# Second layer: the weight words' absolute value moved from ScalarE to VectorE, and a ring of eight tiles for results that DMA adds to DRAM

## The chip, the cores and the metric

The kernel runs on one core of a Trainium2 chip. The metric is the device time of one execution in microseconds, the median of several runs. The kernel before takes 573.15 us (three runs, 572.9 to 574.02).

## The reference

Retention-like attention over 768 steps feeds two feed-forward layers in a row, all in fp32:

```python
state = gamma * state + k_t (outer) v_t            # batch 2, heads 8, head_dim 64
y_t = scale * q_t @ state
x = y as (1536 tokens, 512)
h = x @ w_in;  x = (h * clip(h + 3, 0, 6) / 6) @ w_out         # first layer, d_ff 2048
h = x @ w_in2; out = (h * tanh(softplus(h))) @ w_out2          # second layer, d_ff 2048
```

The weights reach the kernel as 64-bit words. On the chip, five elementwise steps make an fp32 tile from the two 32-bit halves of each word.

## The kernel before

Tokens form three blocks of 512, of which blocks 1 and 2 are mostly worked on together. A product in near-fp32 accuracy is three matmul passes over a high and a low part of each operand; ScalarE casts the high part ("gh", "wdh", "wsh": a CAST) and VectorE subtracts to get the low part ("gl", "wdl", "wsl"). Quadrants of the matrices are combined so that a pair of blocks (or two halves of block 0) needs seven products in place of eight ("up_pair", line 774, "pair_down", line 954).

The second layer (layer 1) runs from about 300 us to the end, in four groups g of two weight pairs each. A group has an **up stage**, in which the products go to the PSUM tiles wx and wy, and a **down stage**, in which they go to the PSUM tiles acc. In the up stage ScalarE copies a first product out of wx or wy (the snap, line 811), VectorE adds others to it (line 814), and ScalarE applies Mish (line 731) in place or straight from PSUM. Products of a pair of blocks are 512 columns wide ("w"); those of block 0 are 256 wide ("v"). TensorE cannot reuse wx before the snap has left it. The down stage has two parts, "block" (b) and "pair" (p); AFTER (line 58) says for each group which comes first.

The down stages of groups 0 to 2 leave 16 results each, four from the block and twelve from the pair. ScalarE copies each out of acc ("copied", line 921; 48 copies in all) into one of four tiles, sb00 to sb03 in turn. From there a DMA writes it to a DRAM tile "part": the first time plainly, from SP's queue (line 933, 12 DMAs), later with an addition, from GpSimd's queue (line 935, 36 DMAs). Two of a group's copies get another product added in the tile by VectorE (line 927) before they leave. A copy into an sb tile therefore waits until the DMA of the copy four before it has read that tile. Two results of each group are joined by VectorE in the sb tile before they leave (line 927).

While a group runs, the weights of the next are prepared: two halves per pair, "cvu" for up and "cvd" for down. Each half starts with the absolute value of the high words, an ACTIVATE with function Abs on ScalarE (line 444), followed on VectorE by a clamp (446), a shift with mask (448) and two merges with the raw words (449, 451). One cvu, one cvd and two raw buffers exist. Abs and Mish are in different function tables here: in the second layer an ACT_TABLE_LOAD stands wherever ScalarE goes from the one to the other.

The order of all instructions is made by a planner ("Plan.order", line 130): each step has an engine, an estimated time, its inputs, its buffers and a rank, and the engine takes the ready step of the lowest rank. ScalarE, VectorE, GpSimd and SP run their own queues strictly in that order, so a step that waits holds up those behind it.

Of the kernel before, what the change touches and what calls it, by code (L numbers as in the profile page):

```python
# [11 lines left out]
F32 = mybir.dt.float32  # L12
# [3 lines left out]
AF = mybir.ActivationFunctionType  # L16
ALU = mybir.AluOpType
# [3 lines left out]
P = 128  # L21
# [33 lines left out]
FREE = 1.5  # L55
ISSUE, ADDED = 1.0, 5.7
ORDER = (1, 5, 6, 3, 7, 2, 4)
AFTER = ("bp", "bp", "pb", "pb")
BORDER = {"pb": (2, 3, 0, 1), "bp": (0, 1, 2, 3)}
KPV = 1  # L60

# [1 line left out]
def dve(n, two=True):  # L63
    return 0.15 + n * (1.045e-3 if two else 0.525e-3)


def act(n, bias=False):
    return 0.17 + n * 0.86e-3 + (0.09 if bias else 0.0)
# [30 lines left out]
class Plan:  # L99
# [3 lines left out]
    def add(self, nm, eng, dur, deps, bufs, emit, rank=None):  # L103
        bufs = list(dict.fromkeys(getattr(b, "base", b) for b in bufs))
        t = Task(nm, eng, dur, deps, bufs, emit, rank)
        t.idx = len(self.tasks)
        self.tasks.append(t)
        for b in bufs:
            if not b.users:
                t.new.append(b)  # L110
                b.owner = t
            elif b.owner not in t.deps:
                t.deps.append(b.owner)
            b.users.append(t)
        for d in t.deps:
            d.succ.append(t)
        return t
# [87 lines left out]
def body(ctx: ExitStack, tc: tile.TileContext, aps: dict, out: bass.AP):  # L205
    nc = tc.nc
# [3 lines left out]
    fix = ctx.enter_context(tc.tile_pool(name="fix", bufs=1))  # L210
# [12 lines left out]
    def buf(pool, shape, tag, dt=F32):  # L223
        count[0] += 1
        name = f"{tag}_{count[0]}"

        def make():
            if pool == "post" and "post" not in pools:
                att.close()
                pools["post"] = ctx.enter_context(tc.tile_pool(name="post", bufs=1, reuse_waits="tile"))  # L230
            return pools[pool].tile(shape, dt, tag=tag, name=name, bufs=BUFS.get(tag, 1))
        return Buf(tag, make)
# [7 lines left out]
    V, A = nc.vector, nc.scalar  # L240
    pl = Plan()
    add = pl.add
# [29 lines left out]
    for n, what in enumerate(LOADS.split() + [f"{x}{u}" for u in range(NU) for x in ("qk", "kv")]  # L272
# [4 lines left out]
        elif what[0] == "t":  # L277
            if what not in lds:
                c = int(what[1:])
# [62 lines left out]
    def seq(key, us):  # L342
        pe_rank[key] = clock[0]
        clock[0] += us
# [16 lines left out]
    def sq_up(u):  # L361
        seq(u, {"c": 12 * MMR, "w": 6 * MMR, "v": 6 * MMH}[u[0]])
        up_end[u] = clock[0]
# [28 lines left out]
    for g in range(NG):  # L392
        for nxt in flow1[g]:
            sq_up(nxt)
        for what in AFTER[g]:
            if what == "b":
                for f in range(g * 2 * NP, (g + 1) * 2 * NP):
                    for d in BORDER[AFTER[g]]:
                        seq(("bd", f, d), 3 * MMR)
# [20 lines left out]
    def words_of(layer, p, half, cb, parts):  # L420

        rb = buf("fix", [P, 1024], "raw", I64)
        src = aps["w1" if layer == 0 else "w2"][p, half]

        def part(k):
            n = 1024 // parts
            cs = slice(k * n, (k + 1) * n)
            nm = f"w{layer}_{p}_{half}{k}"
            ld = add(nm, "SP", DMA512 * n / 512, [], [rb],
                     lambda: nc.sync.dma_start(out=rb.tile[:, cs], in_=src[:, cs]))  # L430
            ld.after = ld_w[0]
            ld_w[0] = ld

            def words():
                w = rb.tile.bitcast(I32).rearrange("p (n t) -> p n t", t=2)
                return w[:, cs, 0], w[:, cs, 1]

            def c():
                return cb.tile[:, cs]

            def ci():
                return cb.tile.bitcast(I32)[:, cs]
            a0 = add(nm + "abs", "ACT", act(n), [ld], [rb, cb],
                     lambda: A.activation(c(), words()[1].bitcast(F32), AF.Abs))  # L444
            a1 = add(nm + "c", "DVE", dve(n, False), [a0], [cb],
                     lambda: V.tensor_scalar(c(), c(), TOP_MAX, TOP_MIN, ALU.min, ALU.max))
            a2 = add(nm + "t", "DVE", dve(n, False), [a1], [cb],
                     lambda: V.tensor_scalar(ci(), ci(), 3, 0x3FFFFFF8, ALU.logical_shift_left, ALU.bitwise_and))
            a3 = add(nm + "o1", "DVE", dve(n), [a2], [cb, rb], lambda: V.scalar_tensor_tensor(
                out=ci(), in0=words()[0], scalar=29, in1=ci(), op0=ALU.logical_shift_right, op1=ALU.bitwise_or))  # L450
            return add(nm + "o2", "DVE", dve(n), [a3], [cb, rb], lambda: V.scalar_tensor_tensor(
                out=ci(), in0=words()[1], scalar=-0x40000000, in1=ci(), op0=ALU.bitwise_and, op1=ALU.bitwise_or))
        return part
# [76 lines left out]
    xt, x32, tform = {}, {}, {}  # L530
# [386 lines left out]
    added = {}  # L917
    taken = [0]
    back = {}

    def copied(nm, ac, dep, rk):
        taken[0] += 1
        tp = buf("fix", [P, 512], f"sb0{taken[0] % 4}")
        return tp, add(f"ev{nm}", "ACT", act(512), [dep], [ac, tp], lambda: A.copy(tp.tile, ac.tile), rk)  # L924

    def joined(nm, ac, tp, cs, deps, rk):
        return add(f"ev{nm}", "DVE", dve(cs.stop - cs.start), deps, [ac, tp], lambda: V.tensor_tensor(
# [2 lines left out]
    def into_part(nm, tp, b, d, dep):  # L930
        pt = part[b, d]
        if (b, d) not in added:
            added[b, d] = add(f"pw{nm}", "SP", 0.8, [dep], [tp, pt], lambda: nc.sync.dma_start(out=pt.tile, in_=tp.tile))
        else:
            added[b, d] = add(f"pa{nm}", "POOL", ADDED, [dep, added[b, d]], [tp, pt], lambda: nc.gpsimd.dma_start(  # L935
                out=pt.tile, in_=tp.tile, accum_op=ALU.add))

    def read_back(b):
# [15 lines left out]
    def pair_down(g):  # L954
# [34 lines left out]
        def rank_after(k, d):  # L989
            later = [pe_rank["pd", g, n, ps[0], d] for n in ORDER[ORDER.index(k) + 1:] if banks[n] == banks[k]]  # L990
            if not later and AFTER[g] == "bp":
                return up_end[flow1[g][-1]] + 40.0
            return (later[0] if later else pe_rank["bd", ps[0] * 2, banks[k][d]]) - DVE1 - LAT
        for k in ORDER:
# [21 lines left out]
            for d in range(2):  # L1016
                ac, rk, nm = accs[banks[k][d]], rank_after(k, d), f"{g}_{k}_{d}"
                dd = 2 * half + d
                if final:
                    into_back(nm, ac, b, dd, [last[d]], rk, k in (3, 7, 2, 4))  # L1020
                    ev[banks[k][d]] = back[b, dd][1] if k not in (3, 7, 2, 4) else []
                elif k == 3:
                    tp, t = kept[d]
                    t = joined(nm, ac, tp, slice(0, 512), [last[d], t], rk)
                    into_part(nm, tp, b, dd, t)
                else:
                    tp, t = copied(nm, ac, last[d], rk)
                    ev[banks[k][d]] = [t]
                    if k == 6:
                        kept[d] = (tp, t)  # L1030
                    else:
                        into_part(nm, tp, b, dd, t)

    def block_down(g):
        fs = range(g * 2 * NP, (g + 1) * 2 * NP)
        final = g == NG - 1
        accs = [buf("acc", [P, 512], f"acc{d}") for d in range(4)]
        prev = {}
        for f in fs:
            gb, tg = gval[1, f, 0]  # L1040
            gh, gl, tl = split(f"b{f}", gb, tg)
            wh, wl, wt = wdown[1, f]
            for d in BORDER[AFTER[g]]:
                ends = f == NFT - 1 and d == 1
                for n, cs in enumerate((slice(0, 256), slice(256, 512)) if ends else (slice(0, 512),)):
                    prev[d, n] = add(f"B{f}_{d}{n}", "PE", 3 * (MMH if ends else MMR), [tl, wt, prev.get((d, 0))],
                                     [wh, wl, gh, gl, accs[d]], lambda d=d, cs=cs, f=f, wh=wh, wl=wl, gh=gh, gl=gl: passes(
                                         accs[d], wh, wl, d * P, gh, gl, f == fs[0], f == fs[-1], cs),
                                     pe_rank["bd", f, d] + 0.36 * n)
                    if f == fs[-1] and final:  # L1050
                        into_back(f"b{f}_{d}{n}", accs[d], 0, d, [prev[d, n]], None, True, cs)
        if not final:
            for d in BORDER[AFTER[g]]:
                rk = pe_rank["pd", g, ORDER[d // 2], g * NP, d % 2] - DVE1 - LAT
                if AFTER[g] == "pb":
                    rk += 33.0
                tp, t = copied(f"b{g}_{d}", accs[d], prev[d, 0], rk)
                into_part(f"b{g}_{d}", tp, 0, d, t)
# [107 lines left out]
```

## Time and profile before

| | |
|---|---|
| median of three runs | 573.15 us |
| the profiled execution, its time | 574.66 us |
| its span on the core | 572.9 us |
| PE (TensorE) busy | 542.8 us, 95% |
| DVE (VectorE) busy | 467.8 us, 82% |
| ACT (ScalarE) busy | 367.7 us, 64% |
| POOL (GpSimd) busy | 34.3 us, 36 adding DMAs |
| mean granted clock of TensorE | 0.987 |

Busy time is the sum of instructions of an engine. "Idle before" of an instruction is how long its engine stood still ahead of it, and the name behind the arrow is what ended that wait by the profile. [...] Neighbouring instructions of one engine overlap a little, so the distance from one start to the next counts, not the duration.

### The profile page before, as it was taken

The numbers are of one execution on the slowest core, as the hardware profiler recorded it, in microseconds if no ns is written. First come the engines' busy times: TensorE is split into PE (matmuls) and PEld (weight loads), VectorE is DVE, ScalarE is ACT, GpSimd is POOL, SyncE is SP. The second block draws the span as 40 slices with busy tenths as digits, with TensorE's granted clock in tenths as the row PEclk, the third lists the DMA queues.
The fourth block names the chain that finished last, engine by engine and source line by source line (L and its number), as shares of the span: only waits on it lengthen the run. The fifth ranks groups of instructions, "written<-read, shape, count | busy, mean of one in ns | idle before, by whom it ended". The sixth has DMA issues, their size and how long they took to land.

```text
span 572.9 us, 8389 instructions
## 1 busy us (share of the span) xinstructions
PE 542.8 (95%) x3139; PEld 454.4 (79%) x3139; DVE 467.8 (82%) x745; ACT 367.7 (64%) x661; POOL 34.3 (6%) x40
## 2 busy tenths in 40 slices
PE   7899999999999999999998989998995999988997
PEld 6788888888898888888886878877884887766985
DVE  4799998699758993799999879978994888857693
ACT  4898645666545552557548868778865869566540
POOL 0000000000000000000000000200242004320000
PEclk9999999999999999999999989999999899998999
DMA  8987423022400422022210043643289327964223
GB/s 343 405 311 251 147 74 128 21 74 74 146 1 1 148 74 73 1 73 74 77 72 2 0 148 146 126 169 116 62 126 234 51 74 153 192 97 148 74 108 112
DMA packets 19768, 67.43 MB, mean 118 GB/s; under 512 B 2192, under 2 KB 2448, under 8 KB 15888
## 3 DMA queue, kind: packets, MB, share of 16 engines
q1 hardware_dynamic: 14544, 57.47, 28.0%
q0 software_dynamic: 5184, 9.44, 11.3%
q8 instruction: 24, 0.39, 0.3%
q14 instruction: 16, 0.13, 0.1%
HBM read 51.17 MB, written 15.73 MB: 117 GB/s over the span
## 4 chain that ended last, share of the span: by engine, by line
PE 69%; issue 11%; DMA 8%; ACT 7%; DVE 2%; POOL 2%; DVEq 0%; SPq 0%; POOLq 0%; ACTq 0%
PE acc L238 38%; PE wx L238 18%; PE wy L238 14%; DMA part<-sb 3%; DMA qk<-in_qk_dram 3%; POOL part L935 2%; ACT L731 1%; ACT L444 1%; DMA kv<-in_kv_dram 1%; ACT cvd L444 1%; ACT g L731 1%; ACT gs L731 1%; ACT sb L924 0%; DVE g L964 0%; DVE gs L814 0%
## 5 line engine op out<-in xcount | busy, mean ns | idle before, releaser
L238 PE MATMUL acc<-gh,wdh 128*128 128x512 f32 x264 | 103.2, 391 | 0.0
L238 PE MATMUL acc<-gh,wdl 128*128 128x512 f32 x264 | 102.9, 390 | 0.0
L238 PE MATMUL acc<-gl,wdh 128*128 128x512 f32 x264 | 102.7, 389 | 0.0
L935 POOL DMA_DIRECT2D part<-sb x36 | 34.1, 981 | 473.9 <-ACT sb L924 436.5
L238 PEld LDWEIGHTS acc<-gl,wdh 128*128 128x128 f32 x264 | 49.6, 188 | 10.5
L238 PEld LDWEIGHTS acc<-gh,wdh 128*128 128x128 f32 x264 | 49.7, 188 | 10.0 <-DVE q L1065 0.3
L238 PEld LDWEIGHTS acc<-gh,wdl 128*128 128x128 f32 x264 | 49.6, 188 | 9.4
L855 DVE TENSOR_TENSOR gl<-g,gh 128x512 fp32r<-128x512 f32 x56 | 38.5, 687 | 16.0 <-ACT gh L853 13.9
L853 ACT CAST gh<-g 128x512 fp32r<-128x512 f32 x56 | 34.9, 623 | 21.2 <-PE acc L238 14.2
L924 ACT COPY sb<-acc 128x512 f32<-128x512 f32 x48 | 28.0, 591 | 13.7 <-DMA part<-sb 9.3
L853 ACT CAST gh<-gs 128x512 fp32r<-128x512 f32 x30 | 18.7, 622 | 15.3 <-PE acc L238 14.5
L855 DVE TENSOR_TENSOR gl<-gs,gh 128x512 fp32r<-128x512 f32 x30 | 20.6, 687 | 8.5 <-ACT gh L853 7.6
L238 PE MATMUL acc<-gh,sb 128*128 128x512 f32 x88 | 27.2, 390 | 0.0
L727 ACT ACTIVATE t<-g,bias 128x512 f32<-128x512 f32 (+1 forms) x22 | 14.6, 666 | 17.8 <-DVE g L814 13.0
L458 ACT CAST wdh<-cvd 128x512 fp32r<-128x512 f32 x32 | 19.5, 621 | 9.4 <-PE acc L238 6.1
L460 DVE TENSOR_TENSOR wsl<-cvu,wsh 128x1024 fp32r<-128x1024 f32 x14 | 17.1, 1221 | 10.1 <-ACT wsh L458 10.1
L460 DVE TENSOR_TENSOR wdl<-cvd,wdh 128x512 fp32r<-128x512 f32 x32 | 21.7, 686 | 3.9 <-ACT wdh L458 3.8
L506 DVE TENSOR_TENSOR cvu<-cvu 128x256 f32<-128x256 f32 x56 | 23.5, 420 | 0.4
L238 PE MATMUL wx<-q,wsh 128*128 128x512 f32 x56 | 22.9, 409 | 0.4 <-DVE q L689 0.4
L444 ACT ACTIVATE cvu<-raw 128x1024 f32<-128x1024 f32 (+1 forms) x17 | 18.6, 1096 | 5.9 <-DMA raw<-in_w_dram 2.1
L238 PE MATMUL wy<-xbh,wsh 128*128 128x512 f32 x56 | 21.9, 391 | 0.0
L238 PE MATMUL wy<-xbh,wsl 128*128 128x512 f32 x56 | 21.8, 390 | 0.0
(234 smaller groups left out, 1553.9 us busy)
## 6 DMA issues: line engine op xcount, KB each, us to landing
raw<-in_w_dram SPq DMA_DIRECT2D x30, 1024.0 KB, 4.9
part<-sb POOLq DMA_DIRECT2D x36, 256.0 KB, 5.4
kv<-in_kv_dram SPq DMA_DIRECT2D x12, 516.0 KB, 7.2
qk<-in_qk_dram SPq DMA_DIRECT2D x12, 512.0 KB, 7.3
part<-sb SPq DMA_DIRECT2D x12, 256.0 KB, 2.0
raw<-in_w_dram SPq DMA_DIRECT2D x4, 512.0 KB, 10.0
qtab<-in_tabs_dram SPq DMA_DIRECT2D x5, 256.0 KB, 8.8
xah<-part SPq DMA_DIRECT2D x4, 256.0 KB, 3.6
```

Source lines behind the costliest of these rows:

```text
L238: nc.tensor.matmul(o, l, r, start=start, stop=stop, skip_group_check=True)
L444: lambda: A.activation(c(), words()[1].bitcast(F32), AF.Abs))
L458: lambda: A.copy(hb.tile[:, h0:h0 + n], cb.tile[:, c0:c0 + n]))
L460: return add(nm + "lo", "DVE", dve(n), [a], list(dict.fromkeys([cb, hb, lb])), lambda: V.tensor_tensor(out=lb.tile[:, l0:l0 + n], in0=cb.t ...
L506: prev = [add(nm + f"s{o}", "DVE", dve(256), prev, [cb], lambda o=o, x=x, y=y, op=op: V.tensor_tensor(out=q(o), in0=q(x), in1=q(y), op=op))]
L727: lambda: A.activation(tb.tile[:, cs], src.tile[:, cs], AF.Relu, bias=bias3))
L731: lambda: A.activation(gb.tile[:, cs], src.tile[:, cs], AF.Mish))
L853: a = add(f"hi{nm}", "ACT", act(512), deps + [prev_split[0]], [gb, gh], lambda: A.copy(gh.tile, gb.tile))
L855: lambda: V.tensor_tensor(out=gl.tile, in0=gb.tile, in1=f32(gh.tile), op=ALU.subtract))
L924: return tp, add(f"ev{nm}", "ACT", act(512), [dep], [ac, tp], lambda: A.copy(tp.tile, ac.tile), rk)
L935: added[b, d] = add(f"pa{nm}", "POOL", ADDED, [dep, added[b, d]], [tp, pt], lambda: nc.gpsimd.dma_start(out=pt.tile, in_=tp.tile, accum_op ...
```

## The change

Three edits.

1. For the second layer, the first step of both weight halves is no longer an ACTIVATE with Abs on ScalarE but a VectorE TENSOR_SCALAR that masks the sign bit of the integer words (16 halves; the first layer keeps Abs).
2. The ring for copied results has eight tiles: sb00 to sb03, a tile with the tag "t", one with the tag "qc", and two halves of a tile with the tag "q". The three new ones are memory that the input forms of the second layer (T1 to T4) used, so a copy also depends on those forms, and on the DMA that last read its tile ("landed").
3. Group 2 has the block part first and the pair part second, as groups 0 and 1 (AFTER).

```diff
-AFTER = ("bp", "bp", "pb", "pb")
+AFTER = ("bp", "bp", "bp", "pb")
...
-            a0 = add(nm + "abs", "ACT", act(n), [ld], [rb, cb],
-                     lambda: A.activation(c(), words()[1].bitcast(F32), AF.Abs))
+            if layer == 0:
+                a0 = add(nm + "abs", "ACT", act(n), [ld], [rb, cb],
+                         lambda: A.activation(c(), words()[1].bitcast(F32), AF.Abs))
+            else:
+                a0 = add(nm + "abs", "DVE", dve(n, False), [ld], [rb, cb],
+                         lambda: V.tensor_scalar(ci(), words()[1], 0x7FFFFFFF, None, ALU.bitwise_and))
...
+    spares, landed = [], {}
+
     def copied(nm, ac, dep, rk):
+        if not spares:
+            wide = buf("fix", [P, 1024], "q")
+            spares.extend([buf("fix", [P, 512], f"sb0{d}") for d in range(4)] + [buf("fix", [P, 512], "t"), buf(
+                "fix", [P, 512], "qc"), View(wide, 0, 512), View(wide, 512, 512)])
+        tp = spares[taken[0] % len(spares)]
         taken[0] += 1
-        tp = buf("fix", [P, 512], f"sb0{taken[0] % 4}")
-        return tp, add(f"ev{nm}", "ACT", act(512), [dep], [ac, tp], lambda: A.copy(tp.tile, ac.tile), rk)
+        forms = [tform[1, w][n][2] for w in "wv" for n in ("T1", "T2", "T3", "T4")]
+        return tp, add(f"ev{nm}", "ACT", act(512), [dep, landed.get(tp)] + sum(forms, []), [ac, tp],
+                       lambda: A.copy(tp.tile, ac.tile), rk)
```

In "into_part" the DMA task is now also kept as landed[tp].

The planner makes another order of it. Three places follow. The first is ScalarE's queue at the end of group 1's down stage, before the change: sb00 to sb03 are the ring, acc the accumulators, g0 and g1 tiles of the next up stage.

```order
L924 COPY sb01_812_4231<-acc2_806_4195 128x512
L731 ACT_TABLE_LOAD
L731 ACTIVATE g0_823_4224<-g0_823_4224 128x512
L924 COPY sb02_813_4247<-acc3_807_4203 128x512
L853 CAST gh_844_4250<-g0_823_4224 128x512
L924 COPY sb03_818_4260<-acc0_774_4020 128x512
L458 CAST wsh0_272_4264<-cvu_268_4072 128x1024
L811 COPY g1_824_4273<-wx_820_4077 128x512
L924 COPY sb00_819_4277<-acc1_775_4029 128x512
```

And with the change:

```order
L936 COPY sb02_689_3409<-acc0_761_4000 128x512
L857 CAST gh_791_4141<-g0_730_3598 128x512
L936 COPY sb03_690_3427<-acc1_762_4008 128x512
L857 CAST wbh1_793_4156<-gs0_737_3750 128x512
L936 COPY t_691_3441<-acc2_785_4137 128x512
L936 COPY qc_692_3445<-acc3_786_4147 128x512
L936 COPY q_686_3475<-acc0_761_4000 128x512
L936 COPY q_686_3475<-acc1_762_4008 128x512
L815 COPY g0_798_4205<-wx_795_4187 128x512
```

Each of these four copies goes to a tile that the copy four before it used, and one of them stands ahead of the snap into g1 (L811). Now the last six copies go to six different tiles, and none of these is used again within eight copies.

The second place is ScalarE's queue in the up stage of group 1, where a cvd half of the next group begins; before:

```order
L811 COPY wsh_753_3737<-wx_3719 128x256
L444 ACT_TABLE_LOAD
L444 ACTIVATE cvd_3818<-raw_3666 128x1024
L731 ACT_TABLE_LOAD
L731 ACTIVATE gs_748_3826<-wx_3692 128x512
```

The same Mish with the change:

```order
L735 ACTIVATE gs_740_3794<-gs_740_3794 128x512
L735 ACTIVATE gs_737_3750<-gs_737_3750 128x512
L735 ACTIVATE gs_738_3783<-gs_738_3783 128x512
L735 ACTIVATE gs_739_3836<-wx_3728 128x512
L735 ACTIVATE wsh_744_3696<-wx_3681 128x256
```

Two table loads and the Abs went out of the row; the whole of ScalarE's order has two table loads left of 22, one at the start and one ahead of the first Mish.

The third place is VectorE's queue for the cvu half before that; before:

```order
L506 TENSOR_TENSOR cvd_3473<-cvd_3473 128x256
L446 TENSOR_SCALAR cvu_3741<-cvu_3741 128x1024
L506 TENSOR_TENSOR cvd_3473<-cvd_3473 128x256
L448 TENSOR_SCALAR cvu_3741<-cvu_3741 128x1024
L506 TENSOR_TENSOR cvd_3473<-cvd_3473 128x256
L449 SCALAR_TENSOR_TENSOR cvu_3741<-raw_3670,cvu_3741 128x1024
```

With the change:

```order
L510 TENSOR_TENSOR cvd_3511<-cvd_3511 128x256
L448 TENSOR_SCALAR cvu_3771<-raw_3674 128x1024
L510 TENSOR_TENSOR cvd_3511<-cvd_3511 128x256
L859 TENSOR_TENSOR gl_3785<-wsh_744_3696,gh_3773 128x512
L510 TENSOR_TENSOR cvd_3511<-cvd_3511 128x256
L450 TENSOR_SCALAR cvu_3771<-cvu_3771 128x1024
```

One TENSOR_SCALAR that reads the raw words was put in ahead of the clamp, and a low part of a down product (gl) now stands among the weight steps.

## Rows read from the trace of the kernel before

**Rows 1.** Busy us by stretch: length, PE, PEld, DVE, ACT, POOL; granted clock, DMA share, GB/s

```profile
250.00:300.00 50.00, 50.00 (x260) 42.61 (x259) 48.23 (x75) 27.96 (x46) 0.00 (x0) 1.00 0.25 85
300.00:505.00 205.00, 189.30 (x916) 157.00 (x915) 170.87 (x274) 155.96 (x252) 32.17 (x34) 0.98 0.49 114
```

**Rows 2.** Timeline of PE: start, duration, instruction, [idle before <-releaser]; the longest stop

```profile
443.72 0.79 PE L238 MATMUL wx<-xbl,wsh 128*128 128x512 f32 x1 [5.92 <-ACT g L811]
```

**Rows 3.** Timeline of ACT: the group's first copies, and two ahead of that stop

```profile
409.96 1.95 ACT L924 COPY sb<-acc 128x512 f32<-128x512 f32 x3
...
437.71 0.59 ACT L924 COPY sb<-acc 128x512 f32<-128x512 f32 x1 [2.95 <-DMA part<-sb]
...
441.65 0.59 ACT L924 COPY sb<-acc 128x512 f32<-128x512 f32 x1 [2.83 <-DMA part<-sb]
```

**Rows 4.** Busy time by stretch, the three in which the granted clock falls

```profile
330.00:340.00 10.00, 8.23 (x44) 7.52 (x44) 8.24 (x12) 6.79 (x15) 0.00 (x0) 0.83 0.35 113
440.00:450.00 10.00, 6.28 (x16) 5.01 (x17) 4.20 (x6) 8.29 (x11) 2.63 (x3) 0.66 0.86 134
520.00:530.00 10.00, 7.90 (x31) 6.22 (x30) 9.06 (x15) 5.37 (x11) 0.00 (x0) 0.83 0.58 210
```

**Rows 5.** Timeline of PE, eight further stops from 300 us on

```profile
317.42 0.50 PE L238 MATMUL wx<-xbl,wsh 128*128 128x512 f32 x1 [0.71 <-ACT gs L811]
...
332.58 0.38 PE L238 MATMUL wx<-xcl,wsh 128*128 128x256 f32 x1 [1.77 <-ACT wsl L811]
...
378.89 0.38 PE L238 MATMUL wx<-xch,wbh 128*128 128x256 f32 x1 [0.83 <-ACT g L731]
...
395.04 0.38 PE L238 MATMUL wx<-xch,wbh 128*128 128x256 f32 x1 [2.20 <-ACT gs L731]
...
462.07 0.38 PE L238 MATMUL wx<-tv,wsh 128*128 128x256 f32 x1 [1.11 <-ACT wsh L811]
...
482.31 0.73 PE L238 MATMUL acc<-wbh,sb 128*128 128x512 f32 x2 [0.54 <-ACT sb L924]
...
516.24 0.50 PE L238 MATMUL wx<-t4h,wbh 128*128 128x512 f32 x1 [1.68 <-DVE g L814]
...
524.11 0.60 PE L238 MATMUL wx<-xbl,wsh 128*128 128x512 f32 x1 [2.10 <-ACT gs L811]
```

**Rows 6.** Timeline of ACT ahead of the stop at 395 us

```profile
390.65 1.28 ACT L444 ACT_TABLE_LOAD   x1
...
394.39 0.60 ACT L731 ACTIVATE gs<-wx 128x512 f32<-128x512 f32 x1
```

**Rows 7.** Groups by line, ACT: busy us, mean ns, idle before and releasers

```profile
L444 ACT ACTIVATE cvu<-raw 128x1024 f32<-128x1024 f32 (+1 forms) x17 | 18.6, 1096 | 5.9 <-DMA raw<-in_w_dram 2.1 <-DVE wsl L460 2.0 <-DVE tv L460 1.1
...
L731 ACT ACT_TABLE_LOAD x11 | 14.1, 1283 | 0.2
...
L444 ACT ACT_TABLE_LOAD x10 | 12.8, 1283 | 0.8 <-DMA raw<-in_w_dram 0.6
```

**Rows 8.** Groups by line and form, DVE

```profile
L449 DVE SCALAR_TENSOR_TENSOR cvu<-raw,cvu 128x1024 int32<-128x1024 int32 x15 | 18.3, 1221 | 0.1
...
L460 DVE TENSOR_TENSOR wsl<-cvu,wsh 128x1024 fp32r<-128x1024 f32 x14 | 17.1, 1221 | 10.1 <-ACT wsh L458 10.1
```

**Rows 9.** Timeline of DVE: the shift with mask of one half, and the next instruction

```profile
324.10 0.69 DVE L448 TENSOR_SCALAR cvu<-cvu 128x1024 int32<-128x1024 int32 x1
324.70 0.69 DVE L689 TENSOR_TENSOR qc<-qc,tv 128x512 fp32r<-128x512 f32 x1
```

**Rows 10.** The page's DMA queues: the queue of the adding DMAs

```profile
q0 software_dynamic: 5184, 9.44, 11.3%
```

**Rows 11.** Timelines of POOL and DVE: two adding DMAs being issued, and a TENSOR_SCALAR

```profile
417.03 1.18 POOL L935 DMA_DIRECT2D part<-sb  x1 [1.05 <-issue]
418.91 0.86 POOL L935 DMA_DIRECT2D part<-sb  x1 [0.70 <-ACT gh L853]
...
417.37 0.76 DVE L448 TENSOR_SCALAR cvd<-cvd 128x1024 int32<-128x1024 int32 x1
```

More of the change, by code (lines that the diff above doesn't have):

```diff
@@ L932, in into_part @@
         if (b, d) not in added:
-            added[b, d] = add(f"pw{nm}", "SP", 0.8, [dep], [tp, pt], lambda: nc.sync.dma_start(out=pt.tile, in_=tp.tile))
+            landed[tp] = added[b, d] = add(f"pw{nm}", "SP", 0.8, [dep], [tp, pt], lambda: nc.sync.dma_start(out=pt.tile, in_=tp.tile))
         else:
-            added[b, d] = add(f"pa{nm}", "POOL", ADDED, [dep, added[b, d]], [tp, pt], lambda: nc.gpsimd.dma_start(
+            landed[tp] = added[b, d] = add(f"pa{nm}", "POOL", ADDED, [dep, added[b, d]], [tp, pt], lambda: nc.gpsimd.dma_start(
                 out=pt.tile, in_=tp.tile, accum_op=ALU.add))
```

## The prediction

> **What bounds the kernel now.** I read the busy time by stretches first. Up to 300 us TensorE never stops; in the second layer, from 300 to 505 us, it stands still for 205 − 189.3 = 15.7 us, and VectorE is busy 170.9 of 205 us (83%) [rows 1]. So TensorE sets the time, and what can be won are its stops and the stretches at a lowered clock. The timeline of TensorE then shows the stops, and nearly all end on ScalarE. The longest, 5.92 us at 443.72, ends with a snap (L811) [rows 2]. ScalarE's timeline shows why the snap was late: two copies into ring tiles stand ahead of it and wait 2.95 and 2.83 us for the DMA that is still reading the tile [rows 3]. ScalarE's queue is in order, so TensorE waits for a DMA that it has nothing to do with. Eight further stops come to 0.71 + 1.77 + 0.83 + 2.20 + 1.11 + 0.54 + 1.68 + 2.10 = 10.9 us [rows 5]. Ahead of the one at 395 us stand a table load, an Abs and a second load, from 390.65 to the Mish at 394.39: 3.74 us in which ScalarE serves nobody [rows 6]. The same triple, or one load of it, stands ahead of the other seven; in the stop at 516 us the load delays a split that VectorE waits for, so the profile names VectorE. [...]
>
> **Part 1, the ring.** It takes away the two DMA waits on ScalarE, and with them the stop of 5.92 us. The clock behind it costs (1 − 0.66) × 6.28 us of busy time = 2.1 us [rows 4]. Together **8.0 us**. What is late next would be the ring of eight itself. The adding DMAs occupy 11.3% of the span, 64.7 us for 36, or 1.8 us each of all 16 DMA engines [rows 10]. Eight copies further on, a tile's DMA has had at most seven others beside it, 7 × 1.8 = 12.6 us; fifteen of group 1's sixteen copies start between 409.96 and 441.65 us [rows 3], which is 25.9 us without the two waits, so eight take 13.8 us, and I cost the wait at nothing. The cover is thin, 1.2 us; without it the copies would wait a few times for that much, behind "part" again, at L936. The new dependence on the forms is free, since the forms are made before the first group's products and the first copy comes after them.
>
> **Part 2, Abs off ScalarE.** Gone are 20 of 22 table loads, 20 × 1.28 = 25.7 us, and 16 Abs of 1.10 us, 17.5 us [rows 7]: 43 us of ScalarE's time. Most of that lay beside TensorE's work. What reaches the end are the eight stops, 10.9 us, and two clock stretches, (1 − 0.83) × 8.23 = 1.4 and (1 − 0.83) × 7.90 = 1.3 us. Together **13.6 us**. ScalarE is then some 60% busy, and nothing there needs a price.
>
> **Part 3, what VectorE gets.** Sixteen TENSOR_SCALAR of 1024 elements. The trace has no TENSOR_SCALAR that reads raw's strided words, so there are two ends. The nearest row is the shift with mask, the same operation and size on packed integers: 0.69 us, and 0.60 from its start to the next start (324.10 to 324.70) [rows 9]. The far end is 1.22 us, a two-input operation. I take the near end, because L449 reads those same strided words at 1.221 us, just as L460 needs 1.221 us for two packed inputs [rows 8]: the stride cost nothing there. [...]
>
> So 16 × 0.60 = 9.6 us more for VectorE. Three of the sixteen stand ahead of 300 us, where VectorE is 48.2 of 50 us busy and makes the forms that the first products of the layer wait for [rows 1]; I count those in full, 1.8 us. Of the other thirteen, 7.8 us, ten or so lie between 300 and 505 us. There VectorE had 34.1 us of idle time. That stretch gets shorter by about 16 us and takes in 6 us, which leaves some 12 us idle: 94% busy. An in-order engine at 94% will make others wait now and then, and half of the 7.8 us, 3.9 us, is my estimate for what shows. Lastly the wait for the weight load moves from ScalarE (2.1 us on cvu [rows 7]) to VectorE, where low parts for the down products stand behind it; 1 us. Together **6.7 us** (ends: 1.8 us where all thirteen are hidden, and 16 × 1.14 + 1 = 19.2 us where the far end holds and all of it shows; 1.14 is 1.22 less the overlap).
>
> **Part 4, block first in group 2.** It adds no instruction. The block needs the v products with their Mish, high and low part; the order has these v products pulled between the w products of groups 1 and 2, so their chain lies beside TensorE's work. Nothing; if the cover fails, one Mish, cast and subtraction, some 2 us.
>
> **Sum.** 8.0 + 13.6 − 6.7 = 14.9 us less. The profiled execution took 574.66 us (span 572.9), which is 1.5 us over the median of the runs, so an execution like it would take 559.8 and the median **558.2 us**.
>
> **Rivals.**
> *VectorE takes back what ScalarE gives.* For it: VectorE at 94%, and stops at 516 and 524 us that already hang on it. Against it: most stops end on ScalarE, with VectorE idle. Then only the ring's 8.0 us stay: 565.2 us. Chance 0.15.
> *All stops go and VectorE's work is hidden.* For it: 34.1 us of idle time, and idle waits of VectorE on ScalarE (10.1 us at L460 [rows 8]) that go as well. 573.15 − 21.6 = 551.6 us. Chance 0.12.
> *Slower: VectorE becomes the end of every stage.* Place: the weight chain, abs to wsl, in front of each up stage. It decides if VectorE's idle time is structural, waits that stay whatever ScalarE does: then each abs pushes the whole queue. At 0.60 us each, 9.6 − 8.0 = 1.6 us are lost, 574.8 us; at 1.14 us, 18.2 − 8.0 = 10.2, 583.4 us. The point is 0.5 us per abs. Against it speaks that the idle time in front of L460 is a wait for ScalarE. Chance 0.05.
> *VectorE holds up the adding DMAs.* A mechanism of this kernel: the DMA issued at 417.03 us, with a TENSOR_SCALAR at 417.37, took 1.18 us, the next one without 0.86; the TENSOR_SCALAR took 0.76 us in place of 0.69 [rows 11]. With more of them, up to 16 issues of a group would each be 0.32 us later, 5.1 us in a down stage; that is more than the 1.2 us of the ring's cover, copies wait again and the ring's gain goes: 558.2 + 8.0 = 566.2 us. Chance 0.04. [...]
> *The change does nothing.* The order shows two table loads left and eight tiles in use, so only a ring and a ScalarE that never mattered would do it; 573 us. Chance 0.02.
>
> **Numbers.** The forecast's chance is 0.62. Its range goes from 551 (the second rival, near) to 568 us, which takes in the first and fourth rivals; the abs at the far end with half of the thirteen showing costs 3.4 + 7.4 + 1 = 11.8 us, 563.4 us, and is inside. Left out are the slower case, doing nothing, and misses of size: about 2 in 10. I go to 549 below, as a stop of group 3 at the first Mish may shrink too. Faster by over 0.2% (1.1 us, about what this measurement can tell from no change): 0.62 + 0.15 + 0.12 + 0.04 = 0.93. Within it: 0.02. Slower: 0.05.
>
> **What would show it.** Right: two ACT_TABLE_LOADs; no idle time at the ring copies for "part"; no stop of TensorE over 2.5 us; a granted clock of 1.00 between 400 and 500 us; the new TENSOR_SCALAR at about 0.69 us; VectorE over 90% busy from 300 us on; stops that are left name VectorE. Wrong: abs at 1.2 us; waits at L936 on DMA; stops of TensorE in front of wx that end on L818 or on the weight chain; a time above 566 us.

## The result and the profile after

| | before | changed kernel |
|---|---|---|
| median on the same chip | 573.02 us (4 runs) | **549.91 us** (4 runs, 548.87 to 550.98) |
| ratio, with its 95% interval | | **0.9605** (0.9565 to 0.9645) |
| span of the profiled execution | 572.9 us | 548.2 us |
| mean granted clock of TensorE (1.00 is full speed) | 0.987 | 0.998 |

The change saves 23.1 us. The forecast was 558.2 us with a range of 549 to 568: the time lies inside, at the low end, and nearest to the second rival (551.6 us, all stops go and VectorE's work is hidden).

The page of the changed kernel, busy time of each engine and the chain that ended last:

```profile
PE 535.1 (98%) x3139; PEld 451.9 (82%) x3139; DVE 475.5 (87%) x761; ACT 328.5 (60%) x625; POOL 33.2 (6%) x40
...
PE 88%; DMA 5%; DVE 3%; ACT 3%; issue 1%; SPq 0%; DVEq 0%; ACTq 0%
```

VectorE has 16 instructions more (761 for 745), ScalarE 36 fewer (625 for 661: 16 Abs and 20 table loads). TensorE is now busy for 98% of the span. Its busy time by stretches (length, PE, PEld, DVE, ACT, POOL; granted clock, DMA share, GB/s), the first two as in [rows 1] and the third as in [rows 4]:

```profile
250.00:300.00 50.00, 50.00 (x258) 42.39 (x258) 49.17 (x78) 25.52 (x45) 0.00 (x0) 1.00 0.24 85
300.00:505.00 205.00, 202.01 (x1011) 170.71 (x1010) 191.67 (x309) 138.56 (x246) 33.01 (x36) 1.00 0.56 129
440.00:450.00 10.00, 8.85 (x45) 7.22 (x44) 9.97 (x15) 6.08 (x11) 0.00 (x0) 1.00 0.07 9
```

In 205 us of the second layer TensorE stands still for 3.0 us, where it was 15.7 [rows 1], and gets through 1011 records of matmuls in place of 916. VectorE is busy for 191.67 of 205 us, 93.5%; 94% was forecast. The granted clock is 1.00 in all three, also where it had fallen to 0.66 [rows 4]. The table of TensorE's waits from 300 us to the end (line waited for; total us, times, longest) has no stop left that is longer than 1.1 us:

```profile
PE wx L238 <- DVE gs L818: 1.1, 1, 1.1
PE wx L238 <- ACT g L815: 0.9, 1, 0.9
PE acc L238 <- DVE sb L464: 0.8, 1, 0.8
PE wx L238 <- DVE q L693: 0.5, 1, 0.5
PE acc L238 <- ACT sb L462: 0.5, 1, 0.5
PE wx L238 <- ACT t2h L691: 0.3, 1, 0.3
PE wx L238 <- ACT gs L735: 0.2, 1, 0.2
```

That is 4.3 us against the 5.92 us of one stop [rows 2] and the 10.9 us of eight more [rows 5]. By the two profiled executions the gain splits cleanly. TensorE's idle time fell from 572.9 − 542.8 = 30.1 to 548.2 − 535.1 = 13.1 us, 17.0 us less, and its busy time for the same 3139 matmuls by 7.7 us; together 24.7 us, the difference of the spans. Of the 17.0 us, 1.0 us lies ahead of 300 us; from there to the end TensorE stood still for 272.90 − 248.72 = 24.2 us before and for 248.20 − 239.98 = 8.2 us now, 16.0 us less (columns as above, before and after):

```profile
300.00:572.90 272.90, 248.72 (x1207) 206.57 (x1205) 217.52 (x350) 189.69 (x308) 34.09 (x36) 0.97 0.46 112
300.00:548.20 248.20, 239.98 (x1208) 202.85 (x1206) 224.01 (x363) 153.84 (x274) 33.01 (x36) 1.00 0.51 123
```

The groups by line and form of VectorE (busy us, mean ns | idle before, releaser) show the new instruction, and what became of the wait in front of "wsl":

```profile
L464 DVE TENSOR_TENSOR wsl<-cvu,wsh 128x1024 fp32r<-128x1024 f32 x14 | 17.1, 1220 | 0.9 <-ACT wsh L462 0.9
...
L448 DVE TENSOR_SCALAR cvu<-raw 128x1024 int32<-128x1024 int32 x8 | 5.5, 687 | 1.7 <-DMA raw<-in_w_dram 1.7
L448 DVE TENSOR_SCALAR cvd<-raw 128x1024 int32<-128x1024 int32 x8 | 5.5, 687 | 0.4 <-DMA raw<-in_w_dram 0.4
```

The masking of strided words takes 687 ns, what the shift with mask takes on packed ones [rows 9]. VectorE's wait for ScalarE's cast in front of "wsl" went from 10.1 us [rows 8] to 0.9 us. A second wait is gone as well, that of the clamp for the Abs on ScalarE, 9.2 us from 300 us on in the kernel before (its table of VectorE's waits; total us, times, longest):

```profile
DVE cvd L446 <- ACT cvd L444: 6.6, 5, 1.9
DVE cvu L446 <- ACT cvu L444: 2.6, 2, 2.1
```

### The profile page after: what moved, and what is told of

The parts are those of the page before. It is cut to its first block, busy times and chain, and to the rows that moved or that the text cites. A ratio compares the mean times of both kernels' runs of the same rounds, so it can differ in the third digit from the quotient of the medians.

```text
span 548.2 us, 8335 instructions
## 1 busy us (share of the span) xinstructions
PE 535.1 (98%) x3139; PEld 451.9 (82%) x3139; DVE 475.5 (87%) x761; ACT 328.5 (60%) x625; POOL 33.2 (6%) x40
## 4 chain that ended last, share of the span: by engine, by line
PE 88%; DMA 5%; DVE 3%; ACT 3%; issue 1%; SPq 0%; DVEq 0%; ACTq 0%
PE acc L238 46%; PE wx L238 23%; PE wy L238 18%; DMA qk<-in_qk_dram 4%; DMA kv<-in_kv_dram 1%; ACT kp L577 0%; DVE gs L818 0%; DVE cvd L510 0%; ACT L735 0%; DVE qc L688 0%; ACT xch L1083 0%; DVE qs L587 0%; ACT xah L645 0%; DVE sb L464 0%; ACT gs L735 0%
## 5 line engine op out<-in xcount | busy, mean ns | idle before, releaser
L947 POOL DMA_DIRECT2D part<-sb x18 | 16.0, 980 | 437.3 <-ACT sb L936 424.6
L238 PE MATMUL acc<-gh,sb 128*128 128x512 f32 x92 | 28.7, 392 | 1.2 <-DVE sb L464 0.8
L462 ACT CAST wdh<-cvd 128x512 fp32r<-128x512 f32 x32 | 19.5, 620 | 10.2 <-PE acc L238 6.1
L464 DVE TENSOR_TENSOR wdl<-cvd,wdh 128x512 fp32r<-128x512 f32 x32 | 21.7, 686 | 4.3 <-ACT wdh L462 4.2
L238 PEld LDWEIGHTS acc<-gh,sb 128*128 128x128 f32 x92 | 17.3, 188 | 5.5 <-DVE sb L464 1.1
L818 DVE TENSOR_TENSOR g<-wy,g 128x512 f32<-128x512 f32 (+1 forms) x26 | 14.7, 564 | 7.8 <-PE wy L238 7.4
L462 ACT CAST wsh<-cvu 128x1024 fp32r<-128x1024 f32 x14 | 14.7, 1047 | 10.1 <-DVE cvu L510 10.0
```

The source lines that it names most:

```text
L238: nc.tensor.matmul(o, l, r, start=start, stop=stop, skip_group_check=True)
L462: lambda: A.copy(hb.tile[:, h0:h0 + n], cb.tile[:, c0:c0 + n]))
L464: return add(nm + "lo", "DVE", dve(n), [a], list(dict.fromkeys([cb, hb, lb])), lambda: V.tensor_tensor(out=lb.tile[:, l0:l0 + n], in0=cb.t ...
L818: return add(f"c{k}_{nm}", "DVE", dve(n), deps, [ps, gb], lambda: V.tensor_tensor(out=gb.tile[:, gc], in0=ps.tile[:, pc], in1=gb.tile[:, g ...
L947: landed[tp] = added[b, d] = add(f"pa{nm}", "POOL", ADDED, [dep, added[b, d]], [tp, pt], lambda: nc.gpsimd.dma_start(out=pt.tile, in_=tp.t ...
```

## The experiments

The prediction's sum is set against its rivals: that VectorE's new work is hidden, that VectorE takes the gain back, that one part alone does all. Ratios are to the kernel before on the same chip, and times of experiments on different chips are compared through these ratios, 1% being 5.73 us. Diffs are against the changed kernel, except where said.

### The parts alone and in pairs

**Ring alone**: Abs back on ScalarE in both layers, the old AFTER.

```diff
-AFTER = ("bp", "bp", "bp", "pb")
+AFTER = ("bp", "bp", "pb", "pb")
...
-            if layer == 0:
+            if True:
```

> Ring of eight alone: Abs stays on ScalarE with its table loads, group 2 keeps the pair first. Theory S (the parts of the change add up, and VectorE's new work costs nothing): the two copies that wait for 'part' and the stop of 5.92 us go, with the lowered clock behind it, 8 us less: about 565 us; the eight stops that end on table loads stay. Rival T (the ring matters only once ScalarE has time: its queue stays late, and the freed waits fill with table loads): 570 us or more, and a stop of several us stays near 440 us.

Measured: 566.87 us, 0.9921 (0.9899 to 0.9943), 4.5 us less. What ended the idle time of ScalarE ahead of its ring copies (us, times), in the view by source line, L924 of the kernel before:

```profile
  DMA part<-sb: 9.3, 7
  PE acc L238: 2.9, 5
  PE wx L238: 1.2, 2
```

The same view of this run, L936:

```profile
  PE acc L238: 5.3, 8
```

The DMA is gone from the list, so the ring does what it says. Yet it gives about half of the 8.0 us. In the place of the longest stop there is a new one. ScalarE's timeline in this run:

```profile
442.32 1.28 ACT L445 ACT_TABLE_LOAD   x1 [1.76 <-DMA raw<-in_w_dram]
443.61 1.12 ACT L445 ACTIVATE cvu<-raw 128x1024 f32<-128x1024 f32 x1
444.75 1.28 ACT L735 ACT_TABLE_LOAD   x1
446.05 1.15 ACT L735 ACTIVATE g<-g 128x512 f32<-128x512 f32 x2
447.10 0.57 ACT L815 COPY gs<-wx 128x512 f32<-128x512 f32 x1
```

And TensorE's, behind that last copy:

```profile
447.72 0.79 PE L238 MATMUL wx<-t2h,wsh 128*128 128x512 f32 x1 [4.04 <-ACT gs L815]
```

The snap out of wx is no longer late for a DMA, but for the triple of load, Abs and load ahead of it, which itself waits 1.76 us for a weight load.

**Absolute value alone**: the old ring and the old AFTER (against the kernel before).

```diff
-            a0 = add(nm + "abs", "ACT", act(n), [ld], [rb, cb],
-                     lambda: A.activation(c(), words()[1].bitcast(F32), AF.Abs))
+            if layer == 0:
...
+            else:
+                a0 = add(nm + "abs", "DVE", dve(n, False), [ld], [rb, cb],
+                         lambda: V.tensor_scalar(ci(), words()[1], 0x7FFFFFFF, None, ALU.bitwise_and))
```

> Absolute value on VectorE alone: ring of four, group 2 pair first. Theory S: two table loads left, 13.6 us less plus some of the clock: about 559 us; the waits of the copies for 'part' stay, 9 us in all. Rival R (ScalarE runs earlier, so copies come closer together and wait longer for the ring of four): the waits for 'part' grow above 9.3 us, and the time is 562 us or more. Rival V (VectorE takes back half): 563 us, with stops that end on VectorE.

Measured: 558.46 us, 0.9791 (0.9758 to 0.9825), 12.0 us less. The copies still wait 8.3 us for "part", and the longest stop is 2.51 us.

**Absolute value and ring**, the old AFTER:

```diff
-AFTER = ("bp", "bp", "bp", "pb")
+AFTER = ("bp", "bp", "pb", "pb")
```

> Absolute value on VectorE and ring of eight, but group 2 keeps the pair first: the change without its third edit. Theory S: the third edit is worth nothing, 550 us within 1.5 us. Rival B (block first in group 2 carries a part of the gain, by giving the first part of the down stage tiles that are ready earlier): 553 us or more, with a stop of TensorE between 440 and 500 us that the changed kernel does not have.

Measured: 551.5 us, 0.9662 (0.9639 to 0.9684), 19.4 us less; the change has 0.9605. So the block first is worth 0.0057 here, 3.3 us (0.6 to 5.9 by the two intervals). Its place is the start of group 2's down stage; TensorE's timeline of this run, with the pair first:

```profile
457.53 0.50 PE L238 MATMUL acc<-gh,sb 128*128 128x512 f32 x1 [1.47 <-ACT sb L462]
459.10 0.50 PE L238 MATMUL acc<-gh,sb 128*128 128x512 f32 x1 [1.07 <-DVE sb L464]
```

The pair's products begin with the summed down weights ("sb" of L462 and L464), and the second of the group's two tiles of them is just being made. VectorE's timeline of the changed kernel, at the same place:

```profile
458.06 1.22 DVE L464 TENSOR_TENSOR sb<-cvd,sb 128x1024 fp32r<-128x1024 f32 x1 [0.37 <-ACT sb L462]
```

TensorE's timeline of the changed kernel, the first product with these weights:

```profile
466.67 0.62 PE L238 MATMUL acc<-gh,sb 128*128 128x512 f32 x2
```

With the block first the low part of this tile is begun 8.6 us ahead of the first product with such weights.

**Order alone**: only the new AFTER (against the kernel before).

```diff
-AFTER = ("bp", "bp", "pb", "pb")
+AFTER = ("bp", "bp", "bp", "pb")
```

> Block first in group 2 alone: Abs on ScalarE, ring of four. Theory S: 573 us within 2 us. Rival B: 570 us or less. A third way: slower by 2 us or more, as the block's copies of group 2 follow the pair's of group 1 sooner in a ring of four.

Measured: 570.66 us, 0.9995 (0.9969 to 1.0021). Alone the order is worth nothing that can be measured.

**Ring and order**, Abs on ScalarE:

```diff
-            if layer == 0:
+            if True:
```

> Ring of eight and block first in group 2, Abs on ScalarE with its loads: the change without its VectorE part. Alone the ring gave 4.5 us and the third edit 0. Theory S: together 4.5 us. Theory M (parts meet in one wait: each shows in full only when the others are in): 4 to 5 us too, as the table loads still hold ScalarE. Rival: the third edit adds 2 us or more to the ring, as it did beside the VectorE part (3 us), because it belongs to the ring.

Measured: 564.92 us, 0.9903 (0.9864 to 0.9942). A stop of 4.14 us at 451.23 us ends on the snap (L815), as with the ring alone.

**Absolute value and order**, the old ring:

```diff
-        tp = spares[taken[0] % len(spares)]
...
+        tp = buf("fix", [P, 512], f"sb0{taken[0] % 4}")
```

> Absolute value on VectorE and block first in group 2, ring of four. Alone the first gave 12 us. Theory S: 12 us. Theory M: the copies' waits for 'part' stay at 8 us or more, and with block first they fall between the down stages of groups 1 and 2 and into the up stage, so 12 us or less. Rival: the third edit belongs to the VectorE part and gives 3 us more: 15 us.

Measured: 554.11 us, 0.9702 (0.9671 to 0.9733), 17.1 us less: its third expectation, that the order belongs to the VectorE part, comes nearest. The copies wait 6.6 us for "part".

The gain of each combination, 1 minus the ratio, in per cent:

| ring | abs | order | ring, abs | ring, order | abs, order | all |
|---|---|---|---|---|---|---|
| 0.79 | 2.09 | 0.05 | 3.38 | 0.97 | 2.98 | 3.95 |

The parts help one another. The ring is worth 0.79 alone and 0.97 beside the other two, a difference within the intervals; beside the absolute value alone it is 1.29. The absolute value is worth 2.09 alone and 2.98 (17.1 us) beside ring and order. The order shows nothing alone and 0.18 beside the ring, within the intervals, but 0.89 (5.1 us; 2.5 to 7.7) beside the absolute value: it belongs to that part. The three alone come to 2.93, together they give 3.95.

### What on ScalarE cost the time

**Abs on ScalarE, in the change's order**: order, ring and AFTER stay as the planner made them for the change; only the engine that executes the sixteen steps is another.

```diff
-                         lambda: V.tensor_scalar(ci(), words()[1], 0x7FFFFFFF, None, ALU.bitwise_and))
+                         lambda: A.activation(c(), words()[1].bitcast(F32), AF.Abs))
```

> The changed kernel's order and ring, word for word, but each of the 16 steps is issued as the Abs ACTIVATE on ScalarE at the same place of the program, so that the table loads come back (22). It undoes the cost of part 2 and keeps the new order. Theory S: the loads and the Abs are what ScalarE lost, about 13 us come back: 563 us. Rival O (the new order, made for free ScalarE, is what helps, and the loads lie beside other work): 553 us or less.

Measured: 574.45 us, 1.0044 (1.0021 to 1.0067). The whole gain is gone, 25.2 us, more than either expectation had. The table loads are back, as ScalarE's groups show:

```profile
L735 ACT ACT_TABLE_LOAD x11 | 14.1, 1283 | 0.2
L448 ACT ACT_TABLE_LOAD x10 | 12.8, 1283 | 2.6 <-DMA raw<-in_w_dram 2.4
```

**A copy on ScalarE in its place**: the words are copied with their sign, so the absolute value is left out.

```diff
-                         lambda: V.tensor_scalar(ci(), words()[1], 0x7FFFFFFF, None, ALU.bitwise_and))
+                         lambda: A.copy(c(), words()[1].bitcast(F32)))
```

> As the run before it, but the step on ScalarE is a plain copy, which needs no table: two table loads, 16 steps of 1.1 us on ScalarE, none of the new ones on VectorE. The sign bit is not cleared, so the absolute value is left out. It parts the loads (25.7 us of ScalarE) from the Abs itself (17.5 us). Theory S with the loads as the cause: within 2 us of the changed kernel, 550 to 552 us. Rival W (the 1.1 us of work on ScalarE matters too): 555 us or more.

Measured: 556.16 us, 0.9706 (0.9676 to 0.9737). The copy takes as long as the Abs did (means of 1126 and 1125 ns for cvd and cvu, 1128 and 1133 with Abs) and needs no load: two are left in the whole run, against 22. Between the two runs, on one chip, lie only the 20 loads: 0.0338, **19.4 us**, some 0.97 us each of the 1.28 us that one lasts. The 18 us of copies on ScalarE, against the masking on VectorE, cost 0.0101, 5.8 us. Both prices hold for this order, which was planned without Abs on ScalarE. "Ring and order" above has the same loads and the same Abs in an order planned for them, and is 0.0141, 8.1 us (5.5 to 10.7), below the run with the loads here. So of the 25.2 us, 8.1 us are the order's; in an order of its own, Abs on ScalarE costs 17.1 us, loads and work together. A switch of tables shows in the trace as little more than the 1.28 us of its load: the Abs starts 1.30 us after the load at 390.65 us does, and the Mish at 394.39 us [rows 6] starts 1.29 us after the second load does. The rows between those of [rows 6], in ScalarE's timeline of the kernel before:

```profile
391.95 1.13 ACT L444 ACTIVATE cvd<-raw 128x1024 f32<-128x1024 f32 x1
393.10 1.28 ACT L731 ACT_TABLE_LOAD   x1
```

### What VectorE can bear

**Twice, three times, not at all**: the new instruction issued two or three times, and in the third kernel left out, with the clamp reading the raw words (the absolute value is then left out).

```diff
-                         lambda: V.tensor_scalar(ci(), words()[1], 0x7FFFFFFF, None, ALU.bitwise_and))
+                         lambda: [V.tensor_scalar(ci(), words()[1], 0x7FFFFFFF, None, ALU.bitwise_and) for _ in range(2)][-1])
```

```diff
-                         lambda: V.tensor_scalar(ci(), words()[1], 0x7FFFFFFF, None, ALU.bitwise_and))
+                         lambda: None)
...
-                     lambda: V.tensor_scalar(c(), c(), TOP_MAX, TOP_MIN, ALU.min, ALU.max))
+                     lambda: V.tensor_scalar(c(), words()[1].bitcast(F32) if layer else c(), TOP_MAX, TOP_MIN, ALU.min, ALU.max))
```

> The changed kernel with each of the 16 new VectorE instructions issued twice, in the same place, order otherwise unchanged: 9.6 us more work for VectorE. If half of VectorE's new work shows, as the prediction took it: 554.8 us. If it is hidden as the changed kernel's profile suggests (no stop of TensorE from it): 551 us or less.

> The same, issued three times: 19.2 us more for VectorE, which is more than the 13.3 us that it is idle between 300 and 505 us in the changed kernel. If idle time is the limit: hidden until the idle time is used up, then one for one: 556 to 560 us. If VectorE's waits are structural: 19 us more, 569 us. If still hidden: under 553 us.

> The changed kernel, its order and its ring, without the 16 new VectorE instructions: the clamp reads the raw words itself. The absolute value is left out, nothing is put in its place. It says what the first 9.6 us of VectorE work cost, where the runs with two and three of them say what the next ones cost (8.5 and 19.9 us). Theory F (the change's own VectorE work fitted into idle time, and the limit is reached just behind it): 549 us, within 1 us of the changed kernel. Rival L (VectorE's work costs nearly one for one from the first on): down to what TensorE's own work allows, 545 us or less.

| masking instructions per half | ratio (interval) | against the row above |
|---|---|---|
| 0 | 0.9619 (0.9584 to 0.9653) | |
| 1, the change | 0.9605 (0.9565 to 0.9645) | −0.8 us, within the intervals |
| 2 | 0.9757 (0.9735 to 0.9778) | +8.7 us |
| 3 | 0.9949 (0.9909 to 0.9989) | +11.0 us |

One masking per half is nearly free: by the two intervals at most 2.2 us, by the spans of the two profiled executions 1.0 us (547.2 and 548.2). The second and third, 16 × 0.60 = 9.6 us of VectorE each, show in full within the intervals; the second costs more than either of its expectations had, the third what the one with structural waits had. The busy time from 300 to 500 us (columns as above), with the instruction left out:

```profile
300.00:500.00 200.00, 197.87 (x986) 167.17 (x985) 181.59 (x290) 136.09 (x242) 32.68 (x36) 1.00 0.54 126
```

The same stretch of the changed kernel, with one:

```profile
300.00:500.00 200.00, 197.01 (x981) 166.38 (x980) 186.67 (x301) 135.25 (x240) 33.01 (x36) 1.00 0.55 124
```

With two:

```profile
300.00:500.00 200.00, 193.64 (x959) 162.10 (x958) 189.96 (x305) 130.06 (x232) 31.84 (x35) 1.00 0.51 119
```

With three:

```profile
300.00:500.00 200.00, 187.80 (x917) 155.13 (x916) 189.27 (x304) 123.31 (x220) 28.10 (x31) 0.99 0.45 106
```

VectorE goes from 91% to 93%, then to 95%, and there it stays; from then on TensorE gives way, 197.0 to 193.6 to 187.8 us. VectorE's idle time over the whole span (span less busy time) says why: 79.7 us with none, 72.7 with one, 71.1 with two and 72.7 with three. The first masking went into 7 us of waits; the others found next to none that would give way, and the waits that are left stay. One stop of TensorE shows each step, in the up stage of group 2, for the additions of L818: 0.27 us with none, 1.15 with one, 2.08 with two, 2.82 with three. With three, the third rival is there to be seen. VectorE's timeline of that run:

```profile
460.29 0.69 DVE L818 TENSOR_TENSOR gs<-wy,gs 128x512 f32<-128x512 f32 x1
460.89 2.14 DVE L448 TENSOR_SCALAR cvd<-raw 128x1024 int32<-128x1024 int32 x3
462.94 0.68 DVE L818 TENSOR_TENSOR gs<-wy,gs 128x512 f32<-128x512 f32 x1
463.54 0.69 DVE L450 TENSOR_SCALAR cvd<-cvd 128x1024 f32<-128x1024 f32 x1
464.14 0.68 DVE L818 TENSOR_TENSOR gs<-wx,gs 128x512 f32<-128x512 f32 x1
```

TensorE's timeline of that run, behind it:

```profile
464.88 0.50 PE L238 MATMUL wx<-t4h,wbh 128*128 128x512 f32 x1 [2.82 <-DVE gs L818]
```

The weight steps of the next group stand between the additions that empty wx and wy, and TensorE waits 2.82 us for the last of them.

**The first three on ScalarE**: the three halves that come before the first Mish keep Abs, which costs no table load there.

```diff
-            if layer == 0:
+            if layer == 0 or (p, half) in ((0, 0), (0, 1), (1, 0)):
```

> The changed kernel, but the three halves whose absolute value comes before the first Mish (both of pair 0, the up half of pair 1) stay on ScalarE, where they need no table load; the other 13 are on VectorE. VectorE was 49.2 of 50 us busy there. If those three push the forms, as the prediction had it (1.8 us): 548 us, with smaller stops at 308 to 312 us. If they are hidden, no difference.

Measured: 550.89 us (five runs), 0.9644 (0.9618 to 0.9671). No gain over the change that can be measured, though VectorE has three instructions fewer in the stretch where it is 98% busy.

## Why the prediction was right, and where it was off

**Part 1, the ring: right in its mechanism.** No copy waits for "part" any more and the 5.92 us stop is gone. Alone, it gives 4.5 us and not 8.0, because the triple of load, Abs and load moves into the stop's place (4.04 us). The sum had both parts, and there the reckoning held: ring and absolute value together measured 19.4 us, where Parts 1 and 2 had 21.6 us before VectorE's share. The thin cover was no danger: in the changed kernel the copies' only idle time is 6.5 us for TensorE. (It was also reckoned too thin: fifteen starts have fourteen distances, so eight take 14.8 us and the cover was 2.2 us.) The adding DMAs took 4.8 to 6.3 us to land in the median, by tile, and the ring holds.

**Part 2, the table loads: right.** The eight stops and the two clock stretches went as listed. The trace agrees in size: 16.8 us of stops were forecast with that of Part 1, and TensorE's idle time from 300 us on fell by 16.0. Two of the eight stops were read too simply: ahead of those at 379 and 524 us ScalarE had itself waited for VectorE behind the load (0.36 and 0.76 us, and 2.21 us), so what they owe to the load is not shown by the rows. Two runs in the change's order that differ in the loads alone put 19.4 us on them. They cost so much because the Mish, the snaps and the casts that TensorE waits for stand behind each pair of loads in the same queue: from 300 us on TensorE waits 17.9 us for ScalarE in the run with the loads and 5.3 us in the one without (sums of the tables of its waits).

**Part 3, what VectorE gives back: the step that failed.** It was set at 6.7 us, of which 5.7 us were for the instructions themselves; those measured between nothing and 2.2 us. Two terms were too large. The three halves ahead of 300 us, "counted in full, 1.8 us", cost nothing that shows: leaving them on ScalarE gained nothing. "Half of the 7.8 us" was an estimate for an engine at 94%. The busy share was right, the conclusion was not: the instructions went into some 7 us of VectorE's waits. The prediction has this argument under the second rival and gave it 0.12; leaving the instruction out altogether showed that rival to be the case.

One piece of the evidence named for it, the 10.1 us in front of "wsl", was misread, though. That wait is as short as in the changed kernel where the table loads and the Abs are back on ScalarE in the change's order, and most of it is gone with the ring alone (groups by line and form of these two runs):

```profile
L464 DVE TENSOR_TENSOR wsl<-cvu,wsh 128x1024 fp32r<-128x1024 f32 x14 | 17.1, 1221 | 0.9 <-ACT wsh L462 0.9
L464 DVE TENSOR_TENSOR wsl<-cvu,wsh 128x1024 fp32r<-128x1024 f32 x14 | 17.1, 1219 | 3.4 <-ACT wsh L462 3.4
```

The first line is the run with Abs back on ScalarE, the second the ring alone. So most of the 10.1 us went with the ring and the planner's order, and not with the loads. The wait that the move itself takes away is the clamp's for the Abs, 9.2 us; with the ring alone it is still there (8.4 and 2.3 us over the whole run). The wait for the raw load moved to VectorE as said, 1.7 + 0.4 us; no run parts what it costs in time. How near the limit is, the doubling shows: the next 9.6 us cost 8.7.

**Part 4, the block first: set at nothing, measured 3.3 us** (0.6 to 5.9). The term looked at the v products and their Mish. The other side counts as well, the summed weights that the pair needs first and the block does not. In the kernel before, the order alone changes nothing, and no stop of TensorE ends on the making of these weights. With the absolute value on VectorE and the pair first, two stops do: 1.47 and 1.07 us with the ring, 2.51 and 0.77 us without it.

With the ring, though, the profiled executions do not show the gain as fewer stops. From 300 us on TensorE is idle for 249.8 − 241.5 = 8.3 us with the pair first and for 8.2 us with the block first: the changed kernel has the 1.15 us on L818 instead, and 0.47 and 0.76 us on summed weights in group 3, which still begins with the pair. The spans differ by 1.6 us, and that is TensorE's busy time, 536.6 and 535.1 us. Behind the pair's two stops the granted clock falls, and in the changed kernel it stays at 1.00 (busy time by stretch, pair first, then block first):

```profile
460.00:465.00 5.00, 5.00 (x17) 3.95 (x16) 4.12 (x5) 3.64 (x7) 1.76 (x2) 0.66 0.52 100
460.00:465.00 5.00, 5.00 (x24) 4.14 (x23) 5.00 (x11) 3.33 (x6) 1.90 (x3) 1.00 0.13 16
```

By an estimate from these rows that is (1 − 0.66) × 5.00 = 1.7 us. Whether the rest of the 3.3 us is more than noise stays open.

**The sum.** These 3.3 us and the 3.5 to 5.7 us that Part 3 was too dear come to 6.8 to 9.0 us, around the 8.3 us between forecast and result. Both errors lie on the same side. The time is inside the range by 0.9 us only, and its lower end had been moved to 549 for a stop of group 3 that might shrink, not for Part 4: that the range held is in part luck.

**The rivals.** VectorE taking back ScalarE's gain, or ending every stage, did not come true with one instruction per half, and did nearly in full with three, at 0.9949. VectorE holding up the adding DMAs was not seen in the sum: 36 issues took 33.0 us of POOL's time, where they took 34.1, with 16 masking instructions more. With 48 in place of 16 the mean of the largest group of issues (18 out of the sb tiles) was 1016 ns, against 980 in the changed kernel. Single issues do show what [rows 11] show: in the changed kernel those at 364.09, 412.42 and 472.68 us took 1.25, 1.39 and 1.29 us, each with a new masking that began 0.47 to 0.61 us into it, and 24 of the other 25 that the timeline lists singly took 0.86 to 0.89 us. The issue of 0.86 us in [rows 11] was not without a TENSOR_SCALAR, though: one of L446 ran from 418.64 to 419.32 us, but it had begun 0.27 us before the issue. The three longer issues come to some 1.3 us more than the others would take, where the forecast had up to 16 times 0.32 us.

**The list of signs.** Two table loads, no wait of copies on "part", no stop over 2.5 us from 300 us on, a clock of 1.00, 687 ns and VectorE over 90%: all held. That the stops that are left name VectorE held in part: 2.4 of 4.3 us do. One sign of being wrong is there too, a stop in front of wx that ends on L818, but it is 1.15 us long.

**What stays open.** TensorE's busy time fell by 7.7 us, where the three clock stretches account for 4.8. By an estimate from the mean clocks of the two executions about 6 us are the clock's, (1 − 0.987) × 542.8 = 7.1 less (1 − 0.998) × 535.1 = 1.1; the rest was not itemised. That the absolute value gains less alone (12.0 us) than beside ring and order (17.1 us) lies with the order by the table; through which waits is shown for single stops only, not summed up. No version ran faster than the change by more than the measurement can tell. A cheaper way to make the absolute value, inside the clamp or on GpSimd, was not measured.

## What to carry to other kernels

A short instruction on an engine that is only 64% busy can cost most of its time (here some 0.97 us of the 1.28 us of a table load) where the engine's queue is in order and another engine's inputs stand behind it; two instructions that need different tables were dearer here by the loads (19.4 us) than by the work itself (5.8 us). The idle time of the engine that takes over such work is no fixed sum: part of it can be waiting for the very step that moves, here 9.2 us from 300 us on, and goes away with the move. Before a wait is put down to one part of a change, look at it in the runs with the other parts alone. Issue the moved instruction twice and three times before deciding: where the cost jumps tells how much room is left. Parts of a change that act on the same queue should be measured in pairs too, since one alone can let the other delay take its place, as with the ring alone a stop of 4.04 us took that of the 5.92 us.

## What the runs showed that was not expected

The step from nearly free to full price is sharp: at most 2.2 us, then 8.7, then 11.0 us for equal additions of 9.6 us, with VectorE at 93%, 95% and 95% from 300 to 500 us. And a change of order that is worth nothing in one kernel (0.9995) is worth 3.3 us in one that is some 3% faster, with a granted clock in the profile that falls in one order and not in the other (0.66 and 1.00 from 460 to 465 us).
